# Token sum of pk summed ahead on VectorE, a Strassen product added in one place and taken away in another, the last tile in quarters, and new tables of order: a two-layer attention and FFN kernel on one core

## The chip, the cores and the metric

The kernel runs on one core of a Trainium2 chip. The metric is the device time of one execution in microseconds (us). Executions of one kernel differ by up to 1.7 us, so effects of a few tenths of a microsecond can't be read from times, only from traces.

Words used below: TensorE multiplies matrices, VectorE and ScalarE work on tiles elementwise, PSUM holds the matmul results in 8 banks. The **pitch** of a matmul is the distance from its start to the start of the next when nothing holds it up. A **matmul wait** is what a start-to-start distance has beyond the pitch. I summed such waits from the matmul starts of a trace, from 10 us on, with pitches of 216, 109, 56, 42 and 25 ns for 512, 256, 128, 96 and 1 columns. A **centring pass** subtracts a token's mean, a part of the layernorm.

## The reference

Twice the same block, on 2048 tokens of width 512, 32 heads of 16 features, an FFN of width 1376; all in bf16:

```python
def _A_ref(x, wqkv, wo):                       # linear attention
    q, k, v = split_heads(x @ wqkv)
    phi = lambda t: where(t > 0, t + 1, exp(t)) + 1e-6
    pq, pk = phi(q), phi(k)
    kv  = einsum("bhsd,bhse->bhde", pk, v)
    z   = einsum("bhsd->bhd", pk)              # the token sum
    num = einsum("bhqd,bhde->bhqe", pq, kv)
    den = einsum("bhqd,bhd->bhq", pq, z)[..., None] + 1e-6
    return merge_heads(num / den) @ wo
def _B_ref(x, w1, w2):                         # FFN
    return max(x @ w1, 0) @ w2
x = x + _A_ref(layernorm(x), wqkv, wo);  x = x + _B_ref(layernorm(x), w1, w2)     # twice
```

(Shortened: shapes, types and the setup of the inputs are left out.)

## The kernel before

All operations are listed once. A table then says in which order they are issued, which engine takes those that either may do (a ScalarE, d VectorE), and which PSUM bank each tile gets. The tables are the outcome of an earlier search, so a change of operations comes with new tables.

```python
ORDER = """
17 0 14 12 15 18 13 1 16 19 2 20 22 3 24 4 21 23 25 5 6 ... 32a ... 46d ...
"""                                     # cut: about 1580 entries
BANKS = ("01436013227545647545447755457477567567454276447564227521...")   # cut
```

All matmuls go through one helper, so in the profile they share a line (L540 before, L538 after) and are told apart by their tiles:

```python
def mm_group(mk, reads, writes, dur, name):
    def _emit(e, mk=mk):
        last = None
        for (o, l, r, st, sp, skip) in mk():
            last = e.matmul(o, l, r, start=st, stop=sp, skip_group_check=skip)
        return last
    return g.add(PE, _emit, reads, writes, dur, name=name)
```

The token sum multiplies each block of 128x128 of pk by a column of ones, for 16 tiles of 4 blocks; the result is masked into Zc, from which the denominators come:

```python
def a_z_acc(lo, hi, zb, first):
    ...                                 # cut: src(i, j), block j of tile i of pk
    def mk():
        return [(psv[:, zb, j:j + 1], src(i, j), ones[:, 0:1], first and i == lo and j == 0, i == NT - 1, True)
                for i in range(lo, hi) for j in range(4)]
```

Strassen's scheme replaces 8 block products by 7, with sums of blocks before and after. It is chosen per chunk of 512 tokens: `QSTR` for Q of the second layer, `HSTR` for the first FFN product of each layer:

```python
QSTR=(3,),  HSTR=[(1, 2, 3), (1, 2, 3)]        # cut from the parameters
hs = HSTR[layer // 2]
steps.append((t, None, lambda t=t: b_h_str(t, layer) if t in hs else b_h(t)))
```

The last FFN output tile is finished in two halves, each with its own store:

```python
prod("f4", summed(3), B21S, ("w2t", "b21-11"), c1, L, False)
if tail:
    rem(c1, l1, L, i1)
    out_half(i1, 0, c1)                 # DVE: residual; then the store, halves on SP and ACT
```

## Time and profile before

| what | before |
|---|---|
| time, median of 4 runs | 270.66 us |
| span of the profiled run | 268.3 us |
| TensorE, VectorE, ScalarE busy | 98%, 89%, 74% |
| TensorE's unbroken run of matmuls, start | 9.59 us |
| end of the last matmul's pitch | 265.27 us |
| matmul waits between these | about 2.1 us |

The last row needs a word. The distances give 6.67 us, but 21 matmuls have no record in this trace (1976 of TensorE against 1997 weight loads), and each, nearly all of 512 columns, leaves a false gap of 0.216 us; 6.67 - 21 x 0.216 = 2.1.

The main views of this profile stand in the prediction.

The end of the timeline:

```profile
265.16 0.27 PE L540 MATMUL ps<-w,big 96*128 96x256 bf16 x1
265.48 0.47 DVE L1138 SCALAR_TENSOR_TENSOR xn<-ps,rstdf,xres 128x256 bf16<-128x256 f32 x1
265.98 0.42 SPq L1141 DMA_DIRECT2D out_dram<-xn  x1
```

The last store is issued 0.71 us after the last matmul's pitch ended (265.16 + 0.11).

### The profile page before, as it was taken

To read this page: it belongs to the slowest core of one execution; us is meant where nothing else is said; L and a number is where in the kernel's file an instruction comes from. 1 tells how busy PE (TensorE), PEld (TensorE's weight loads), DVE (VectorE), ACT (ScalarE), POOL (GpSimd) and SP (SyncE) were. 2 spreads that over 40 slices of the span, in tenths; PEclk is the share of its full clock that TensorE was granted. 3 is DMA by queue.
4 is the path that set the end of the run, shared out by engine and by line. 5 is a ranking of instruction groups with operands and counts; after the bars stand their busy time and mean duration, and the time that the engine had idled before them with its cause. 6 is when DMAs were issued, how large, how long until landed. Compare 5 with 4: busy or idle time off the path is not lost.

```text
span 268.3 us, 5363 instructions
## 1 busy us (share of the span) xinstructions
PE 262.3 (98%) x1976; PEld 172.3 (64%) x1997; DVE 238.4 (89%) x650; ACT 199.2 (74%) x434; POOL 18.7 (7%) x30
## 2 busy tenths in 40 slices
PE   7999999999999999999999999999999999999995
PEld 2444454447556878778776664455457688888884
DVE  4999986999989999998999984799889989999884
ACT  3889955999978769688867987889996878725420
POOL 4021000000110002210011000000100100200000
PEclk9999999999999999999999999999999999999999
DMA  6955882245243024402204400224363232202004
GB/s 202 381 121 82 216 286 94 101 67 119 91 123 75 0 42 86 55 0 44 56 2 78 78 5 2 98 81 85 74 157 100 41 76 45 95 2 84 16 1 156
DMA packets 47482, 23.61 MB, mean 88 GB/s; under 512 B 36736, under 2 KB 46048, under 8 KB 47456
## 3 DMA queue, kind: packets, MB, share of 16 engines
q1 hardware_dynamic: 47312, 23.21, 34.1%
q8 instruction: 15, 0.25, 0.4%
q14 instruction: 11, 0.09, 0.1%
q10 hardware_dynamic: 144, 0.07, 0.1%
HBM read 11.21 MB, written 3.15 MB: 53 GB/s over the span
## 4 chain that ended last, share of the span: by engine, by line
PE 95%; DVE 2%; DMA 1%; issue 1%; ACT 0%
PE ps L540 95%; DMA xin<-in_A_x_dram 1%; DVE bst L447 1%; DVE xn L580 0%; DVE xn L1178 0%; PE ps L503 0%; DVE mv L448 0%; DVE Tb L511 0%; DVE xn L1138 0%; ACT lnv L1169 0%; ACT rstd L1171 0%
## 5 line engine op out<-in xcount | busy, mean ns | idle before, releaser
L547 ACT ACTIVATE sqscr<-xres 128x512 bf16<-128x512 f32 x48 | 30.4, 634 | 10.8 <-DVE xres L584 5.9
L522 ACT ACTIVATE escr<-ps 128x512 bf16<-128x512 f32 x52 | 30.7, 609 | 6.8 <-PE ps L540 6.4
L520 ACT ACTIVATE big<-ps 128x512 bf16<-128x512 f32 x52 | 30.9, 613 | 1.4 <-PE ps L540 1.3
L540 PE MATMUL ps<-big,xn 128*128 128x512 bf16 x121 | 29.4, 379 | 0.4
L540 PE MATMUL ps<-gw,big 128*128 128x512 bf16 x121 | 28.9, 379 | 0.4
L1027 ACT ACTIVATE big<-ps 128x512 bf16<-128x512 f32 (+1 forms) x44 | 22.9, 533 | 6.5 <-PE ps L540 5.7
L540 PE MATMUL ps<-Tb,wqkv 128*128 128x512 bf16 x112 | 27.0, 379 | 0.0
L540 PE MATMUL ps<-wqkv,Tb 128*128 128x512 bf16 x91 | 22.7, 379 | 0.7 <-ACT Tb L510 0.3
L526 DVE TENSOR_TENSOR big<-big,escr 128x512 bf16<-128x512 bf16 x52 | 21.2, 421 | 1.5 <-ACT big L520 0.8
L540 PE MATMUL ps<-w2s,big 128*128 128x256 f16 x160 | 22.1, 272 | 0.0
L540 PEld LDWEIGHTS ps<-big,xn 128*128 128x128 bf16 x128 | 12.1, 98 | 13.9 <-issue 0.7
L540 PE MATMUL ps<-w,big 128*128 128x256 f16 (+2 forms) x113 | 20.9, 302 | 0.0
L540 PEld LDWEIGHTS ps<-gw,big 128*128 128x128 bf16 x128 | 12.2, 98 | 13.4 <-issue 0.5
L1010 ACT ACTIVATE ps<-ps 128x512 f32<-128x512 f32 (+1 forms) x29 | 15.0, 518 | 6.5 <-DVE big L1048 2.6
L540 PE MATMUL ps<-w,xin 128*128 128x256 bf16 (+1 forms) x140 | 19.5, 273 | 0.0
L540 PE MATMUL ps<-xn,xin 128*128 128x256 f16 x128 | 19.4, 273 | 0.0
L540 PE MATMUL ps<-Tb,w 128*128 128x512 bf16 x80 | 18.8, 379 | 0.0
L540 PEld LDWEIGHTS ps<-Tb,wqkv 128*128 128x128 bf16 x112 | 10.6, 98 | 12.0 <-ACT escr L522 0.3
L524 DVE TENSOR_SCALAR escr<-escr 128x512 bf16<-128x512 bf16 x52 | 14.4, 286 | 4.3 <-ACT escr L522 4.2
L540 PE MATMUL ps<-xn,w 128*128 128x256 f16 x120 | 18.2, 273 | 0.0
L540 PE MATMUL ps<-Tb,wper 128*128 128x256 bf16 x120 | 18.2, 273 | 0.0
L540 PEld LDWEIGHTS ps<-w2s,big 128*128 128x128 bf16 x160 | 15.5, 98 | 4.0 <-DVE xres L1105 0.4
(166 smaller groups left out, 548.6 us busy)
## 6 DMA issues: line engine op xcount, KB each, us to landing
xn<-rdram SPq DMA_DIRECT2D x32, 128.0 KB
wqkv<-in_A_wqkv_dram SPq DMA_DIRECT2D x3, 512.0 KB, 7.3
xin<-in_A_x_dram SPq DMA_DIRECT2D x3, 512.0 KB, 8.1
out_dram<-xn SPq DMA_DIRECT2D x3, 512.0 KB, 2.8
w<-in_B_w_dram SPq DMA_DIRECT2D x1, 1376.0 KB, 6.6
w<-in_B_w_dram SPq DMA_DIRECT2D x1, 1280.0 KB, 9.8
rdram<-rsp SPq DMA_DIRECT2D x8, 128.0 KB, 1.7
wo<-in_A_wo_dram SPq DMA_DIRECT2D x1, 512.0 KB, 10.6
```

The source lines that it names most:

```text
L447: g.add(DVE, lambda e: e.bn_stats(bst[:, i, :], xin[:, i, :]), [("xin", i)] + list(behind), [("bst", i)], C_DVE_BNST, name="bnst%d" % i)
L520: g.add(ACT, lambda e: e.activation(dst_ap, psv[:, b, :], ACTF.Identity, bias=1.0 + 1e-6, scale=1.0), [("ps", b)], [dst_key], C_ACT_PSUM, ...
L522: g.add(ACT, lambda e: e.activation(escr[:, s, :], psv[:, b, :], ACTF.Exp), [("ps", b)], [("escr", s)], C_ACT_EXP, name=name + "_exp")
L524: g.add(DVE, lambda e: e.tensor_scalar(escr[:, s, :], escr[:, s, :], 1.0, 1e-6, ALU.min, ALU.add), [("escr", s)], [("escr", s)], C_DVE_BF4 ...
L526: g.add(DVE, lambda e: e.tensor_tensor(dst_ap, dst_ap, escr[:, s, :], ALU.max), [dst_key, ("escr", s)], [dst_key], 340.0, name=name + "_phi")
L540: last = e.matmul(o, l, r, start=st, stop=sp, skip_group_check=skip)
L547: g.add(ACT, lambda e: e.activation(sqscr[:, q, :], xres[:, i, :], ACTF.Square, accum_out=dst[:, i:i + 1]), [("xres", i)], [("sqscr", q), ...
L1010: g.add_flex([(ACT, lambda e: e.activation(dst(), psv[:, src, 0:W], ACTF.Identity), cost(C_ACT_PSUM)), (DVE, lambda e: e.tensor_copy(dst() ...
L1027: g.add_flex([(ACT, lambda e: e.activation(out_ap(r, m), pv(b), ACTF.Relu), cost(C_ACT_PSUM)), (DVE, lambda e: e.tensor_scalar(out_ap(r, m ...
```

## The change

The intent: give TensorE less to do where VectorE can take it. (1) In three chunks of the first layer and all four of the second, VectorE adds the four pk tiles of a chunk to one, in fp16, and only that one goes through the one-column matmuls. (2) The first FFN product of the last layer uses Strassen in chunk 0 as well. (3) Q of the second layer no longer does, which frees VectorE. (4) The last half of the last tile becomes two quarters. The tables of order and banks are new throughout.

```diff
-17 0 14 12 15 18 13 1 16 19 2 20 22 3 24 4 21 23 25 5 6 26 27 7 28 8 29 40 30 33 ...
+17 0 14 12 15 18 13 1 16 19 2 20 22 3 24 4 21 23 25 5 6 26 27 7 28 8 33 29 40 30 ...
 (cut: the rest of ORDER, and BANKS)
-QSTR=(3,), ..., ZP=(0, 0), ..., HSTR=[(1, 2, 3), (1, 2, 3)]
+QSTR=(),   ..., ZSUM=[(0, 1, 2), (0, 1, 2, 3)], ..., HSTR=[(1, 2, 3), (0, 1, 2, 3)]
-        def a_z_acc(lo, hi, zb, first):
+        def a_z_acc(t, zb):
+            ...                                     # cut: tiles, keys and src of the chunk
+            if t in ZSUM[cur_layer[0] // 2]:
+                zs = rhi[:].bitcast(F16)
+                hv = big[:].rearrange("p (c t k) -> p c t k", t=NCH, k=512)
+                ks = [("rhi", 0), ("rhi", 1)]
+                g.add(DVE, lambda e: e.tensor_tensor(zs, hv[:, 0:2, t, :], hv[:, 2:4, t, :], ALU.add), keys, ks, 608.0, name="zs%d" % t)
+                g.add(DVE, lambda e: e.tensor_tensor(zs[:, 0, :], zs[:, 0, :], zs[:, 1, :], ALU.add), ks, ks, 340.0, name="zt%d" % t)
+                src, keys = [zs[:, 0, :]], ks[0:1]
             def mk():
+                return [(psv[:, zb, j:j + 1], x[:, 128 * j:128 * j + 128], ones[:, 0:1], t == 0 and k == 0 and j == 0, t == NCH - 1, True)
+                        for k, x in enumerate(src) for j in range(4)]
-            prod("f4", summed(3), B21S, ("w2t", "b21-11"), c1, L, False)
             if tail:
-                rem(c1, l1, L, i1)
-                out_half(i1, 0, c1)
+                for q in range(2):
+                    cols = slice(128 * q, 128 * q + 128)
+                    prod("f4%d" % q, summed(3), B21S[:, :, cols], ("w2t", "b21-11"), c1, cols, False)
+                    rem(c1, l1, cols, i1)
+                    out_part(i1, cols, c1, q)
-                ... eng=(SP, ACT)[hf] ...            # queue of the store
+                ... eng=(SP, ACT, SP)[k] ...
 (cut: an unused path of the token sum on GpSimd, removed)
```

## The prediction

> **What bounds the kernel now.** I read the engine shares first, then the chain of waits, then TensorE's timeline for the pitch of each kind of matmul, and last VectorE and ScalarE by stage. The page's first two parts (busy microseconds, share of the span, instructions; then busy tenths in 40 slices) say that TensorE is never idle at full clock, and that VectorE is close behind:
>
> ```profile
> PE 262.3 (98%) x1976; PEld 172.3 (64%) x1997; DVE 238.4 (89%) x650; ACT 199.2 (74%) x434; POOL 18.7 (7%) x30
> ...
> PE   7999999999999999999999999999999999999995
> ...
> DVE  4999986999989999998999984799889989999884
> ACT  3889955999978769688867987889996878725420
> ...
> PEclk9999999999999999999999999999999999999999
> ```
>
> A busy TensorE is not yet a bound, because the profile models the ends of matmuls. The chain that ended last settles it: by line it is nearly all one matmul helper, and its pieces (start, length, what) run from 5 us to 265 us in blocks with gaps of about 0.05 us.
>
> ```profile
> by line: PE ps L540 94.9%; DMA xin<-in_A_x_dram 0.9%; DVE bst L447 0.9%; issue 0.6%; DVE xn L580 0.3%; DVE xn L1178 0.3%; PE ps L503 0.2%; DVE mv L448 0.2%; DVE Tb L511 0.2%; DVE xn L1138 0.1%; ACT lnv L1169 0.1%; ACT rstd L1171 0.1%
> ...
> 81.63 30.23 PE ps L540 x263
> ...
> 217.48 47.31 PE ps L540 x427
> 264.79 0.02 issue
> 264.81 0.75 DVE xn L580
> 265.56 0.39 DVE xn L1138
> ```
>
> So a matmul costs its pitch, the start of one block to the start of the next over the number of matmuls, not its listed duration. From TensorE's timeline:
>
> ```profile
> 39.80 5.35 PE L540 MATMUL ps<-big,xn 128*128 128x512 bf16 x24
> 44.99 0.38 PE L540 MATMUL ps<-Tb,wqkv 128*128 128x512 bf16 x1
> ...
> 46.72 1.06 PE L540 MATMUL ps<-gw,wqkv 128*128 128x128 bf16 x16
> 47.62 1.03 PE L540 MATMUL ps<-Tb,wqkv 128*128 128x512 bf16 x4
> ...
> 157.52 1.34 PE L540 MATMUL ps<-ones,big 128*128 128x1 bf16 x48
> 158.72 0.60 PE L540 MATMUL ps<-big,Tb 128*128 128x256 f16 x4
> 159.16 1.03 PE L540 MATMUL ps<-Tb,wqkv 128*128 128x512 bf16 x4
> ```
>
> 512 columns: (44.99-39.80)/24 = 216 ns. 256 columns: (159.16-158.72)/4 = 110 ns. 128 columns: (47.62-46.72)/16 = 56 ns. One column: (158.72-157.52)/48 = 25 ns. Counting all matmuls from 9.6 us to the last (575 of 512 columns, 1066 of 256, 36 of 128, 128 of 96 columns at 42 ns, 128 of one column, 8 denominator groups of 0.34 us) gives about 254 us against the 255.7 us that the trace shows. At most 2 us are stalls, and most of them are the small issue gaps. The kernel is a sum of matmul pitches plus a head of 9.6 us and a tail of 3 us.
>
> **What the Trainium skill says.** "TensorE: Matmul & The Clock Gate", section "Wait — 56ns, not 53.3ns?": a warm matmul takes N/2.4 GHz plus about 2.5 ns, and start to start never falls below about 25 ns. The trace agrees to the nanosecond: 216, 110, 56 and 25 ns. So a one-column matmul is nearly half as dear as one of 128 columns, and it is the number of them that counts. "VectorE: DVE Perf Modes", sections on the performance tiers and on the TRN2 errata: tensor_tensor on 16-bit data in SBUF handles two elements a cycle, and a SBUF operation costs 58 cycles and the elements over that rate at 0.96 GHz. That is 327 ns for 512 elements and 727 ns for 1280; in VectorE's timeline such sums start 0.335 and 0.73 us apart, so the trace agrees, and 1024 elements should take 0.60 us. "DMA: Bandwidth & Descriptors", section on the anatomy of one DMA: a fixed cost of about 2 us that doesn't shrink with the size. Here 128 KB landed 1.7 us after issue and 64 KB 1.6 us, so a smaller last store gains next to nothing. Its specification table adds that pieces under 512 B lose rate; quarter-width rows are 256 B. No store of that kind is in this trace.
>
> **The change part by part.**
>
> (1) Token sum of pk. Before, both attention layers sum 16 tiles with 4 one-column matmuls each: 128. After, chunks 0 to 2 of the first and all four of the second are first added on VectorE to one tile, so the matmuls are 3x4 + 16 = 28 and 4x4 = 16. TensorE loses 84 x 25 ns = 2.10 us. VectorE gains seven times one addition of 1024 elements (0.60, estimated above) and one of 512 (0.335): 6.6 us. In itself this lies beside the matmuls.
>
> (2) First FFN product of the last layer, chunk 0, by Strassen. Plain: 10 blocks x 4 = 40 matmuls of 512: 8.64 us. Strassen: 7 products x (4+4+2) = 70 of 256 at 109.4 ns: 7.66 us. TensorE loses 0.98 us. The weight sums exist already (made once in layer 1). Extra on VectorE: four sums of transposed tiles (1.34), three additions c21 and three hadd (0.61 full, 0.34 half size: 1.56 each), three small maxima (0.5): 5.0 us. On ScalarE or VectorE: 9 copies and 9 ReLU, each six full at 0.48 and three half at 0.28 (7.4 us together), in place of 10 ReLU (4.8): 2.6 us more.
>
> (3) Q of layer 2, chunk 3, without Strassen: from 28 x 109.4 ns = 3.06 us to 16 x 216 ns = 3.46: TensorE gains 0.40 us. VectorE is freed of five weight sums and four tile sums (9 x 0.335) and two additions on PSUM (0.6 each): 4.2 us. ScalarE is freed of three copies: 1.45 us.
>
> (4) Tail in quarters. The last half product of 5+1 matmuls of 256 (0.66 us) becomes two of 5+1 of 128 (0.67 us): nothing on TensorE. The end gets longer, as I read the new table of order. The last quarter's matmuls wait until VectorE has read the first quarter from the same bank; the product and remainder of tile 15 fill that wait. But tile 15's own output (0.67 us on VectorE) is placed just ahead of the last quarter's, and only 0.34 us of matmuls follow it. Before, the last store was issued at 265.98 us, 0.7 us after the last pitch ended (about 265.27). After, I get: last pitch T, tile 15's output from T-0.14 to T+0.53, quarter output (about 0.34) to T+0.87, then a store that queues behind that of tile 15 on the same issuer (about 0.4 us per issue in this trace): T+1.0. That is 0.3 us worse, an estimate.
>
> Sum on the path: -2.10 - 0.98 + 0.40 + 0.02 + 0.3 = -2.4 us, so 270.57 - 2.4 = 268.2 us. VectorE: +6.6 + 5.0 - 4.2 = +7.4 us, from 238 to about 246 in a span of 266 (92%). ScalarE: +1.2.
>
> **The rivals.**
>
> VectorE becomes the bound in a stage. Busy time by stretches of the kernel before:
>
> ```profile
> 145.00:165.00 20.00, 19.89 (x176) 12.46 (x177) 17.56 (x55) 17.90 (x36) 1.11 (x1) 1.00 0.14 28
> 165.00:190.00 25.00, 24.84 (x145) 12.40 (x147) 20.65 (x63) 21.39 (x44) 0.00 (x0) 1.00 0.27 75
> 190.00:215.00 25.00, 24.89 (x188) 16.11 (x189) 22.46 (x64) 21.32 (x51) 2.01 (x2) 1.00 0.42 99
> 215.00:240.00 25.00, 24.95 (x227) 21.03 (x226) 23.27 (x59) 16.29 (x38) 2.01 (x2) 1.00 0.23 56
> 240.00:265.00 25.00, 25.00 (x229) 20.84 (x227) 21.18 (x38) 8.36 (x20) 0.00 (x0) 1.00 0.15 53
> ```
>
> Columns after the length are TensorE, its weight load, VectorE, ScalarE, GpSimd. The sums of layer 2 (3.7 us) fall into 145 to 170 us, where 5 us are free and 1.7 us of Q's weight sums go away. The new Strassen chunk puts 5.0 us on VectorE and 2.6 on ScalarE in 190 to 215 us, where 2.5 and 3.7 are free: it doesn't fit there. It must draw on the 4 us free and the 2.5 us freed before, and move work that either engine may do to ScalarE, which has 8.7 us free in the next stretch. In sum it fits. If the order misses, TensorE waits for buffers: 1 to 2 us lost, 269 to 270. Against it: the kernel before runs VectorE above 9.5 of 10 for long stretches and shows hardly a matmul wait.
>
> The token sum sits on the path of its stage. The new order of work is then PSUM, exponential, maximum, two additions, matmul, mask, denominator; if the extra 1 us of latency delays the first denominator and nothing fills the gap, up to 1 us per attention layer comes back: 269 to 270. Against it: projections and accumulation matmuls are there to fill, and in the first layer the last chunk stays unsummed.
>
> The tail is better than I read it, or the whole order is a lucky one: 267.3 to 267.8.
>
> **Range and chances.** The matmul count is certain and its pitch measured, so -2.7 us before the tail is firm; nearly all doubt lies in new stalls, and they only add. Predicted 268.2 us, range 267.3 to 269.7. Faster by over 2% needs 265.2 or less, 3 us beyond what the matmuls can give: 0.02. Slower by over 2% needs over 7 us of new stalls: 0.01. Within 2%: 0.97.
>
> **What would show it.** Right: one-column matmuls 44 instead of 128 and still 25 ns apart; 70 more of 256 columns with FFN operands; VectorE's busy time near 246 us with TensorE's share unchanged; the fp16 additions starting 0.6 and 0.34 us apart; the last store issued about 1.0 us after the last matmul's pitch. Wrong: waits of matmuls for VectorE of over 0.3 us between 195 and 225 us or ahead of the first denominator groups; TensorE pieces in the chain interrupted by VectorE; a gain over 2.7 us, which would mean that the kernel before had hidden stalls that I took for pitch.

## More of the kernel before

The one-column matmuls of the token sum, from the view by tile of `ones` (count, then listed ns as minimum, median, maximum):

```profile
L540 PE MATMUL ps<-ones,big x128: 163/163/177, 18.4 to 163.9; 128*128 128x1 bf16 x128
```

The listed 163 ns is the way through the engine, not the cost: they follow each other at 25 ns. Next, from the timelines of the DMA queue and of TensorE, the transposes of the normalized tiles for the first FFN product, and the matmuls that read them first (start, length, what):

```profile
55.85 6.87 SPq L486 DMA_TRANSPOSE Tb<-xn  x4
...
65.27 2.85 PE L540 MATMUL ps<-Tb,w 128*128 128x512 bf16 x12
```

No idle time is noted in brackets behind the matmuls: the transposes, begun 9 us ahead, had landed.

## The result, and the profile after

| | before | after |
|---|---|---|
| time, median of 4 runs each | 270.66 us (270.08 to 270.93) | 268.37 us (268.26 to 269.12) |
| ratio | | 0.9924 (95%: 0.9899 to 0.9948) |
| the same again, 11 and 6 runs | 270.40 us | 268.80 us, ratio 0.9932 (0.9911 to 0.9954) |
| span of a profiled run | 268.3 us | 267.4, again 266.7 us |

A ratio is the mean time of the one kernel's runs over the mean of the other's runs of the same rounds, so it is not quite the ratio of the medians beside it. The gain is 0.7 to 0.8%, some 2 us, which counts as the same within 2%. The profile of the first line's runs fell on their slowest one (269.12 us), so I read the second profile of the same kernel (run of 268.47 us, all 1937 matmuls recorded). First the page's engine line:

```profile
PE 261.4 (98%) x1937; PEld 171.7 (64%) x1937; DVE 240.5 (90%) x660; ACT 202.3 (76%) x446; POOL 19.6 (7%) x30
```

TensorE is as full as before, with 60 instructions fewer (1997 - 84 + 70 - 40 - 28 + 16 + 6 = 1937: the one-column matmuls, the FFN product, Q, the quarters). VectorE rose by 2 us only. The token sum in the first profile of the changed kernel, by the tiles `ones` and `rhi` (the sums lie in `rhi`):

```profile
L538 PE MATMUL ps<-ones,rhi x28: 163/163/167, 34.2 to 165.0; 128*128 128x1 bf16 x28
L538 PE MATMUL ps<-ones,big x16: 163/163/163, 38.8 to 39.2; 128*128 128x1 bf16 x16
L616 DVE TENSOR_TENSOR rhi<-big x7: 680/686/693, 29.1 to 162.5; 128x1024 f16<-128x1024 bf16 x7
L617 DVE TENSOR_TENSOR rhi<-rhi x7: 417/420/426, 31.4 to 163.3; 128x512 f16<-128x512 f16 x7
```

128 one-column matmuls became 44, and seven pairs of additions came. The same rule of reading holds for VectorE: 686 ns is listed, but the next operation starts 0.60 to 0.61 us later. Two rows of busy time by stretch answer to the prediction's (TensorE, weight load, VectorE, ScalarE, GpSimd after the length):

```profile
145.00:165.00 20.00, 20.00 (x133) 11.27 (x132) 19.24 (x54) 17.89 (x36) 0.00 (x0) 1.00 0.14 28
...
190.00:215.00 25.00, 25.00 (x226) 19.77 (x224) 23.78 (x65) 23.13 (x57) 1.01 (x1) 1.00 0.52 96
```

In the stage of the second token sum VectorE went from 17.56 to 19.24 us of 20, and in the stage of the new Strassen chunk from 22.46 to 23.78 of 25. There is little left of either, and TensorE's column shows no hole. The hole is elsewhere. Pieces of the chain that ended last (start, length, what):

```profile
10.01 49.41 PE ps L538 x272
...
60.53 0.61 ACT xn L556
...
61.47 4.75 DMA Tb<-xn
66.22 0.05 issue
66.27 27.54 PE ps L538 x189
...
93.83 0.76 DVE xres L582 x2
...
102.17 0.38 ACT ps L1104
...
102.59 160.74 PE ps L538 x1288
```

Before, the chain ran through these times in one piece after another of TensorE:

```profile
48.79 10.31 PE ps L540 x49
59.10 0.05 issue
59.16 15.46 PE ps L540 x109
```

Now it leaves TensorE at 59.4 us, goes through a centring pass on ScalarE and the transpose of that tile by DMA, and returns at 66.27. The timelines of the queue and of TensorE show the same:

```profile
55.21 2.87 SPq L484 DMA_TRANSPOSE Tb<-xn  x2
...
60.11 2.62 SPq L484 DMA_TRANSPOSE Tb<-xn  x2
...
66.27 1.90 PE L538 MATMUL ps<-Tb,w 128*128 128x512 bf16 x8 [0.82 <-DMA Tb<-xn]
```

Before, four transposes were issued in one go from 55.85 us. In the new order two of them come at 60.11 us, after a late centring pass, and the matmuls that read them wait (0.82 us idle by the profile, 0.99 us against the pitch). A smaller wait of 0.31 us stands at 102.2 us, at the entry to the first FFN's second product, where the kernel before had 0.09 us; there the chain runs for 8.8 us, from 93.8 to 102.6 us, mostly through VectorE.

**The sum.** From the start of TensorE's unbroken run to the end of the last pitch the kernel before took 265.27 - 9.59 = 255.7 us and the changed one 263.64 - 9.62 = 254.0 us: 1.7 us less. The matmuls removed are worth 2.10 + 0.98 - 0.40 - 0.02 = 2.66 us. So 1.0 us of new waits came, which is what the waits themselves say: 3.2 us against 2.1. Last, the end of the timeline after:

```profile
263.31 0.45 PE L538 MATMUL ps<-w,xin 128*128 128x128 f16 x5
...
263.60 0.22 PE L538 MATMUL ps<-w,big 96*128 96x128 bf16 x1
264.02 0.34 DVE L1134 SCALAR_TENSOR_TENSOR xn<-ps,rstdf,xres 128x128 bf16<-128x128 f32 x1
...
264.40 0.37 ACTq L1138 DMA_DIRECT2D out_dram<-xn  x1
```

The last pitch ends at 263.60 + 0.04; the store follows 0.76 us later, on ScalarE's queue.

### The profile page after: what moved, and what is told of

Read it like the earlier page. It is cut to its first block, busy times and chain, and to the rows that moved or that the text cites. A ratio compares the mean times of both kernels' runs of the same rounds, so it can differ in the third digit from the quotient of the medians.

```text
span 267.4 us, 5269 instructions
## 1 busy us (share of the span) xinstructions
PE 260.0 (97%) x1919; PEld 171.5 (64%) x1937; DVE 240.7 (90%) x660; ACT 202.4 (76%) x446; POOL 19.6 (7%) x30
## 4 chain that ended last, share of the span: by engine, by line
PE 85%; DVE 7%; DMA 5%; issue 1%; ACT 1%; SPq 0%; DVEq 0%
PE ps L538 84%; DMA Tb<-xn 3%; DMA xin<-in_A_x_dram 1%; DVE xres L551 1%; DVE xres L582 1%; DVE ps L1035 1%; DVE xn L970 1%; DVE xin L1061 1%; DVE xn L558 0%; ACT big L518 0%; PE ps L501 0%; DVE xn L578 0%; DVE bst L445 0%; DVE KVT L649 0%; ACT xn L556 0%
## 5 line engine op out<-in xcount | busy, mean ns | idle before, releaser
L520 ACT ACTIVATE escr<-ps 128x512 bf16<-128x512 f32 x56 | 33.3, 614 | 7.1 <-PE ps L538 7.0
L1021 ACT ACTIVATE big<-ps 128x512 bf16<-128x512 f32 (+1 forms) x57 | 29.2, 530 | 8.0 <-PE ps L538 7.7
L518 ACT ACTIVATE big<-ps 128x512 bf16<-128x512 f32 x56 | 33.3, 611 | 1.4 <-PE ps L538 1.3
L538 PE MATMUL ps<-Tb,wqkv 128*128 128x512 bf16 x128 | 30.5, 379 | 0.0
L538 PE MATMUL ps<-xn,w 128*128 128x256 f16 x140 | 21.8, 273 | 0.0
L538 PE MATMUL ps<-w,big 128*128 128x256 f16 (+3 forms) x114 | 21.6, 301 | 0.0
L538 PE MATMUL ps<-Tb,wper 128*128 128x256 bf16 x140 | 21.3, 272 | 0.0
L538 PEld LDWEIGHTS ps<-big,xn 128*128 128x128 bf16 x128 | 12.0, 97 | 13.1 <-issue 0.7
L571 POOL TENSOR_TENSOR rstdf<-varf,nhalf 128x4 f32<-128x4 f32 x8 | 9.6, 1201 | 145.1 <-DVE varf L569 145.1
L538 PE MATMUL ps<-w,xin 128*128 128x256 bf16 (+2 forms) x145 | 19.7, 269 | 0.1
L1104 ACT ACTIVATE ps<-ps 128x256 f32<-128x256 f32 x27 | 10.0, 371 | 11.8 <-PE ps L538 10.3
```

Source lines behind the costliest of these rows:

```text
L518: g.add(ACT, lambda e: e.activation(dst_ap, psv[:, b, :], ACTF.Identity, bias=1.0 + 1e-6, scale=1.0), [("ps", b)], [dst_key], C_ACT_PSUM, ...
L520: g.add(ACT, lambda e: e.activation(escr[:, s, :], psv[:, b, :], ACTF.Exp), [("ps", b)], [("escr", s)], C_ACT_EXP, name=name + "_exp")
L571: g.add(POOL, lambda e: e.tensor_tensor(rstdf[:, sl], varf[:, sl], nhalf[:, 0:4], ALU.pow), [("varf", t), ("nhalf",)], [("rstdf", t)], C_P ...
L1021: g.add_flex([(ACT, lambda e: e.activation(out_ap(r, m), pv(b), ACTF.Relu), cost(C_ACT_PSUM)), (DVE, lambda e: e.tensor_scalar(out_ap(r, m ...
L1104: g.add_flex([(ACT, lambda e: e.activation(psv[:, c1, cols], psv[:, c2, L], ACTF.Identity), 290.0), (DVE, lambda e: e.tensor_copy(psv[:, c ...
```

## The experiments

**Theory.** The time is the sum of the matmul pitches; the change takes 2.66 us of them away, and its new order has about 1.0 us more waits. **Rivals:** VectorE at its limit (the additions cost TensorE time, so their saving is partly given back); the tail in quarters costs or gains; the gain comes from the new order alone and not from the operations. Three calls were made, each with eleven runs of the kernel before beside it (medians 270.40, 270.38 and 270.35 us); ratios are against these.

### The changed kernel again

No edit. It is the baseline of the other runs.

> The changed kernel unaltered, timed again in five rounds as the yardstick for the parts. If the matmul count sets the time and the first profile's 1 us wait for a transposed tile was chance, the ratio to the kernel before is about 0.9915 (2.3 us less) and that wait is absent or shorter. If the wait belongs to the schedule, it shows again near 62 us with about 1 us.

Measured: 268.80 us, ratio 0.9932, as in the table above. The gain is repeatable, and so is the wait for the transpose near 65 us (0.82 us idle by the profile, 1.0 us in the first one): by the expectation's own test it belongs to the order.

### The token sum without the additions

The new order, but every tile goes through the one-column matmuls again:

```diff
-ZSUM=[(0, 1, 2), (0, 1, 2, 3)]
+ZSUM=[(), ()]                       # and the 14 entries of the additions taken out of ORDER
```

> The changed kernel with the pk tiles summed by TensorE again in both layers: 84 one-column matmuls more, seven pairs of VectorE additions (6.6 us) fewer, everything else in its place. Theory (TensorE's count is the bound): 84 x 25 ns = 2.1 us slower than the changed kernel. Rival (VectorE is the bound in the stages of the sums): the freed 6.6 us of VectorE pay part of it back, under 1.2 us slower.

Measured: 271.15 us, ratio 1.0015 (0.9991 to 1.0039), 2.35 us above the changed kernel by the medians; 84 x 25 ns are 2.10 us. All of the token sum's saving arrives, and without it the rest of the change is level with the kernel before. Page line and TensorE's timeline of this run:

```profile
PE 263.7 (98%) x2021; PEld 174.1 (65%) x2021; DVE 234.9 (87%) x646; ACT 202.6 (75%) x446; POOL 19.7 (7%) x30
...
66.62 2.75 PE L537 MATMUL ps<-Tb,w 128*128 128x512 bf16 x12
```

Two things are to be seen. VectorE is 5.6 us less busy, so the seven pairs cost 5.6 us of busy time. And the matmuls that read the transposes start at 66.62 us with no wait for them. Yet its matmul waits sum to 3.1 us, as in the changed kernel: they lie elsewhere (0.8 us at 60 to 70 us, 0.6 us at 190 to 210 us). So the extra microsecond of waits belongs to the new order; the additions didn't bring it.

### The additions kept, the matmuls put back as idle ones

This separates the two halves of that trade. Behind each summed chunk 12 one-column matmuls are added whose results nobody reads, 84 in all:

```diff
+                if len(src) == 1:
+                    mms += [(psv[:, zb, 8 + j:9 + j], src[0][:, 128 * j:128 * j + 128], ones[:, 0:1], False, t == NCH - 1, True)
+                            for r in range(3) for j in range(4)]
```

> The changed kernel with 84 idle one-column matmuls added behind the sums, into columns that nobody reads; VectorE's work is unchanged. Theory: 84 x 25 ns = 2.1 us slower. Rival (the matmuls hide in waits for VectorE or the denominator): under 1 us slower. The difference from the run with direct sums is what the VectorE additions cost by themselves: 0 by the theory.

Measured: 271.19 us, ratio 1.0024 (0.9998 to 1.0050): 2.39 us for 84 matmuls, 28 ns each by the medians, with an uncertainty of about half a microsecond in all. A one-column matmul costs its pitch, end to end. The run differs from the one above only in having the additions and in the operand of the matmuls, and the two medians are 0.04 us apart: 5.6 us of VectorE's busy time cost nothing measurable.

### The larger addition twice

The rival in its own coin: each of the seven sums does its addition of 1024 elements once more.

```diff
+g.add(DVE, lambda e: e.tensor_tensor(zs, hv[:, 0:2, t, :], hv[:, 2:4, t, :], ALU.add), keys, ks, 608.0, name="zr%d" % t)
```

> The changed kernel with the 1024-element addition done twice in each of the seven sums: 4.2 us more VectorE work, TensorE unchanged. Theory (VectorE has room in these stages): within 0.3 us. Rival (VectorE is at its limit there, and the change's own additions already cost time): 1 to 4 us slower, with matmuls waiting for VectorE between 25 and 40 us or 150 and 165 us.

Measured: 272.17 us, ratio 1.0053 (1.0031 to 1.0075), 3.37 us above the changed kernel for 7 x 0.60 = 4.2 us more of VectorE. The waits of matmuls (total us, times, longest):

```profile
PE ps L538 <- DVE rhi L618: 1.0, 2, 0.5
PE ps L538 <- DVE xn L971: 1.0, 1, 1.0
PE ps L538 <- DMA Tb<-xn: 1.0, 1, 1.0
PE ps L538 <- DVE big L524: 0.8, 1, 0.8
```

TensorE now waits for the sums themselves (`rhi`), at 167 us, ahead of the second layer's first denominators, for a phi product on VectorE (`big`) and at 201 us for a sum of transposed tiles (`xn`); the wait for the DMA is the old one. Waits sum to 7.2 us against 3.2. The theory's "within 0.3 us" missed. So the rival is false for the change as it stands and true for 4 us more: the additions just fit.

### The tail in halves

The new order with the last half product in one piece:

```diff
-                for q in range(2):
-                    cols = slice(128 * q, 128 * q + 128)
-                    ...                                   # cut: the quarter's product, remainder, output
+                prod("f4", summed(3), B21S, ("w2t", "b21-11"), c1, L, False)
+                rem(c1, l1, L, i1)
+                out_part(i1, L, c1, 1)
```

> The changed kernel with its last product in one half of 256 columns instead of two quarters, everything else in its place. My prediction took the quarters for 0.3 us of loss, since it had the last store queue behind another on one issuer; the first trace shows it on an issuer of its own, 0.7 us after the last matmul, as before. Theory now: within 0.2 us of the changed kernel, and the 0.16 us wait ahead of the last quarter's matmuls gone. If the first reading was right after all: 0.3 us faster. If the quarters help: 0.2 us or more slower.

Measured: 268.87 us, ratio 0.9935 (0.9909 to 0.9962), against 268.80 and 0.9932. Its end:

```profile
264.05 0.27 PE L538 MATMUL ps<-w,big 96*128 96x256 bf16 x1
...
264.88 0.38 ACTq L1136 DMA_DIRECT2D out_dram<-xn  x1
```

The store follows the last pitch (264.05 + 0.11) by 0.72 us; with quarters it was 0.76. With quarters there is also a wait of 0.17 us ahead of the last product, for VectorE's read of the first quarter from the same bank, which is absent here. So by the traces quarters cost some 0.2 us; in the times no difference shows.

### The token sum alone, in the old order

The kernel before with the seven pairs of additions, each put right behind the last tile it needs; Q, FFN product, tail and the rest of the order as before.

```diff
-a_z_acc over all 16 tiles
+ZSUM=[(0, 1, 2), (0, 1, 2, 3)]      # additions inserted into the old ORDER
```

> The kernel before with the summed pk tiles as the only part of the change, its order otherwise kept. By the matmul count alone: 2.1 us faster than the kernel before. Since doubled additions cost 3.4 us, I now expect VectorE to take most of it back where the order was not made for it: 0 to 1.5 us faster, with matmul waits for VectorE near the sums, and the waits are to show that the new order is a part of the gain.

Measured: 277.51 us, ratio 1.0245 (1.0217 to 1.0273): slower by 7 us, with 2.1 us less work for TensorE. One such place in TensorE's timeline:

```profile
39.43 0.25 PE L537 MATMUL ps<-ones,rhi 128*128 128x1 bf16 x4 [1.57 <-DVE rhi L616]
```

The additions for this chunk ran at 38.15 and 38.95 us, just ahead of the matmuls, which stood in front of all later matmuls in TensorE's queue. Matmul waits sum to 13.1 us. That is 10.9 us more than before; less the 2.1 us of work it makes 8.8 us, as the spans have it (277.1 against 268.3 us).

Not all of that is waiting. TensorE's granted clock, in 40 slices of this run:

```profile
PEclk9999998999999999999999997999999999999999
```

It was half from 40.4 to 43.9 us and from 166.7 to 170.2 us, so about 3 of the 13.1 us are slower matmuls. In the 3.4 us just before each of the two stretches TensorE had been busy for only 1.75 and 1.05 us, held up by the waits. The one run of six with a mean clock of 1.0 took 276.15 us, 5.8 us above the kernel before; the others had 0.988 to 0.994.

So the operations without the order lose, and the order without the additions gains nothing (1.0015, above): the rival "the order alone" falls, and put into the old order this plainly the operations gain nothing.

### The FFN product without Strassen in chunk 0

```diff
-HSTR=[(1, 2, 3), (0, 1, 2, 3)]
+HSTR=[(1, 2, 3), (1, 2, 3)]         # order and banks redone around it by plain list placement
```

> The changed kernel with chunk 0 of the last layer's first FFN product computed plainly again (40 matmuls of 512 columns instead of 70 of 256), banks and order redone only there. Theory (count of matmuls): 1.0 us slower than the changed kernel, about 269.8. Rival (the 5 us on VectorE and 2.6 on ScalarE that Strassen adds cost time in 190 to 215 us): less than 0.5 us slower, or even faster.

Measured: 285.37 us, ratio 1.0542 (1.0516 to 1.0567). Waits rose to 19.5 us (about 3 of them slower matmuls, in two stretches at half clock), nearly all between 180 and 240 us, where I had redone the order. The test is spoiled by my order and tells nothing of the 0.98 us end to end. That figure rests on the count (40 matmuls of 512 columns against 70 of 256) and on the pitches, which are the same in both traces.

### The centring pass and the transposes earlier

The wait at 65 us attacked directly: ten entries of the order moved, so that the late centring pass and its transposes come earlier; all operations unaltered.

```diff
 ORDER: entries of nmf1, cen1, tr0, nmf2, nmf3, cen3, cen2, tr2 and one sum of tiles moved ahead;
        one product (wa1_2) moved behind wa1_1
```

> The changed kernel with ten entries of its order moved: the weight sum wa1_2 behind wa1_1, and the centring of tiles 1 to 3 with their transposing stores ahead of it, so that the second transpose of chunk 0 is issued about 0.8 to 1.2 us earlier. If the 1.0 us wait near 65 us is set by that issue, it shrinks below 0.3 us and the kernel gains 0.7 to 1.0 us: about 267.8. If the wait is set by something else (traffic of other transfers, the producing matmuls), the gain is under 0.3 us.

Measured: 268.58 us, ratio 0.9922 (0.9901 to 0.9944), 0.2 us below the changed kernel's median and within its interval. The wait for the transposes is gone, but see the product ahead of it in TensorE's timeline:

```profile
65.38 0.61 PE L538 MATMUL ps<-xn,xin 128*128 128x256 f16 x4 [0.37 <-DVE nm2f L565]
...
66.26 2.10 PE L538 MATMUL ps<-Tb,w 128*128 128x512 bf16 x9
```

The matmuls that read the transposes start at the same 66.26 us. TensorE now waits elsewhere instead, mostly for VectorE, 1.1 us in this stretch against 1.3. That moving one pass up moved others down, with VectorE busy for 9.6 us of the 10 from 60 to 70 us (in the changed kernel), is argued, not shown: the kernel before has 9.7 us there and no such wait.

### Other orders for the same operations

Could an order searched anew separate the parts? I searched one for the kernel before, for the changed one, for the token sum alone and for the changed one without Strassen in chunk 0, with the kernel's own replay of durations and somewhat slower hand-overs between engines.

> The kernel before, its operations unaltered and only the order of issue searched anew (by the kernel's own replay of its order with slower hand-overs between engines). The kernel before has hardly any matmul waits left, so an order cannot give much: within 0.4 us of it. If it is over 1 us faster, the gain of the change was mostly its new order and not its smaller matmul count.

> The kernel before plus the summed pk tiles alone, order searched as in the run before this one. By the matmul count: 2.1 us faster than the kernel before. If the 6.6 us of additions don't fit VectorE as long as Q of layer 2 is still by Strassen (4.2 us of VectorE work), part is lost again: 0.5 to 1.5 us faster, with matmul waits for VectorE near 160 us.

> The changed kernel with chunk 0 of the last layer's first FFN product plain, order searched in the same way; it takes the place of the earlier attempt, whose order was bad. By the count of matmuls: 1.0 us slower than the next run. If Strassen's extra work on VectorE and ScalarE costs time there: 0.5 us slower or less.

> The changed kernel, its operations unaltered, order searched in the same way. Its matmul waits in the trace come to 1.0 us near 65 us, 0.3 near 102 us and 0.2 us at the end. If the order can hide them: 0.7 to 1.3 us faster than the changed kernel, about 267.7, and the fastest of all. If they only move: within 0.3 us.

| operations | tuned order | order searched anew | ratio of that to before |
|---|---|---|---|
| before | 270.35 us | 281.74 us | 1.0413 (1.0395 to 1.0430) |
| token sum alone | none | 282.32 us | 1.0413 (1.0380 to 1.0447) |
| changed, plain FFN chunk 0 | none | 278.37 us | 1.0304 (1.0262 to 1.0346) |
| changed | 268.80 us | 276.37 us | 1.0215 (1.0195 to 1.0235) |

(The 268.80 us are from the first call.) Where there is a tuned order, mine is slower by 11.4 and 7.6 us. Waits of matmuls in the last run:

```profile
PE ps L538 <- DVE big L524: 3.0, 4, 1.2
```

TensorE waits at 11 to 65 us for the phi products on VectorE (`big`), which my replay had thought ready. By the medians the token sum alone shows no gain over its partner (waits of 14.4 us against 11.9), and the plain FFN chunk is 2 us slower than its partner. But these medians mix clocks. The profiled run of the token sum alone has two stretches of 3.4 us at half clock (8.7 to 12.1 and 25.7 to 29.1 us), and four of its six runs (282.07 to 282.72 us) have a mean clock of 0.988. Its two runs at 0.998 and 1.0 took 279.95 and 280.33 us, the three of its partner at 0.999 or more 281.37 to 281.94 us: about 1.6 us faster, of the 2.1 us of the count. Likewise the plain FFN chunk at 0.999 or more (277.46 to 277.70 us) against its partner at 0.998 or more (275.75 and 276.16 us): 1.6 us slower, where the count says 0.98. So few runs, of orders that differ, agree with the counts in sign but don't prove their sizes; as a clean separation the runs miss. What they do show is the size of the order's part: four to six times that of the whole change.

No run beats the changed kernel clear of noise.

## Why the prediction was right or wrong

Predicted were 268.2 us; 268.37 and 268.80 us came. The total lies within the range in both, and the verdict of the same within 2% held. By its steps:

- **The bound.** Right. TensorE is full in both kernels, and 84 idle matmuls of one column cost about what the pitch says (28 ns each for 25). By the traces the gain was 1.7 us, not 2.4; that the first median lies only 0.2 us from the prediction is in part the luck of the runs, since the second lies 0.6 us off.
- **Token sum, -2.10 us.** Right, shown by two runs (2.35 and 2.39 us). Its cost on VectorE was given as 6.6 us from the start-to-start distances; the busy time rose by 5.6 us.
- **FFN product, -0.98 us, and Q, +0.40 us.** Right as counts at unchanged pitches. No run isolates either end to end: the one for the FFN product was spoiled by its order, and Q was not tried. Nor do the times show them: without the additions the changed kernel is level with the one before, so what these parts save is no more than the new order's waits take back.
- **Tail, +0.3 us.** Mis-sized, and for another reason than given. I wrote that the last store "queues behind that of tile 15 on the same issuer". It is on ScalarE's queue, and tile 15's output starts 0.29 us ahead of the last pitch's end instead of 0.14, so the store comes 0.76 us after it, not 1.0. But I also had the last quarter's wait for its bank filled by tile 15's product and remainder, and 0.17 us of it stays. Together about 0.2 us, and not visible in the times.
- **The failed step: "nearly all doubt lies in new stalls, and they only add", with no term for them in the sum.** About 1.0 us came, 0.17 of it that of the tail. I had looked for them between 195 and 225 us and ahead of the denominators. The largest is at 65 us, in a stage whose operations the change doesn't touch: a late centring pass, a late transpose. I read the order table for the tail only. One of the prediction's own signs of being wrong, the chain leaving TensorE for VectorE, did appear from 93.8 to 102.6 us, but only 0.31 us of waiting came of it. A term of 1 us in place of the tail's 0.3 would have given 270.57 - 2.66 + 1.0 = 268.9 us.
- **Rival "VectorE becomes the bound".** Not at the change's size, but 4.2 us more of it cost 3.4 us. Near, as the figures given there had it: if all of the second layer's additions fall into 145 to 165 us, 17.56 + 3.7 - 1.7 = 19.6 us of 20, and 19.24 was measured. (Free between 145 and 170 us were 6.1 us, not the 5 that the prediction states: 2.44 before 165 us and 3.64 after.)
- **VectorE's busy time, 246 us.** 240.5 us were measured. In part the additions added less than priced (5.6 for 6.6). In part work that either engine may do went to ScalarE: its operations that take a Strassen result from PSUM with ReLU rose from 44 to 57, where the change has only 9 more, and its busy time rose by 3.1 us instead of 1.2.
- **Rival "the token sum sits on the path of its stage".** In the changed order not: between 30 and 50 us, the waits are about what they were. In the old order with the additions put in plainly it happened, with single waits of up to 1.9 us.

What stays open: why just this order has the late centring pass. It came out of a search, and a search that minimizes a modelled time can place a wait where the model sees none; that is argued, not shown.

## What to carry to other kernels

Where TensorE is full, price a change by counting matmuls times pitch, and test that price by adding idle ones: 84 of one column cost 2.4 us. Then read the new order at every place where data comes from another engine or by DMA, in untouched stages too, because a stall costs as much as forty small matmuls and no count shows it. And when a part is undone for an experiment, the order must be remade as well as it was made, or the experiment measures the order: here orders were worth 8 to 11 us and the change 2. And compare runs at the same granted clock: with the token sum alone in the searched order, the runs at a mean clock of 0.988 took 1.7 to 2.8 us longer than those at 0.998 or more, as much as the whole change gains.

## What the Trainium skill lacked or had wrong

- "TensorE: Matmul & The Clock Gate", section "Wait — 56ns, not 53.3ns?": N/2.4 GHz and 2.5 ns with a floor near 25 ns hold here where the granted clock was full, but for the denominators: the four matmuls of such a group, of 512 columns and on 32 columns of the array each, start 3 ns apart. It doesn't say that the floor counts end to end: 84 idle one-column matmuls cost 2.39 us, 28 ns each, in a full TensorE.
- "VectorE: DVE Perf Modes", section on the TRN2 errata: it gives a fixed cost of 58 cycles and, as measured for a single operation, about 150, and this section doesn't say which to use for back-to-back work (another page of the skill does). Both show here: a sum of 1024 elements is listed with 686 ns (659 cycles, 147 above 512) and the next starts after 0.60 to 0.61 us (64 to 74 above).
- "DMA: Bandwidth & Descriptors": beside figures of rate it has no time from issue to landing for an on-chip transpose of a tile of 128x512 (elsewhere the skill has one duration, for 128x128). Here the median is 3.2 us for 30 transposes, and the one that TensorE waited for took 4.75 us in the chain. For its warning on pieces under 512 B: the last stores of 32 KB in rows of 256 B landed 1.6 to 1.7 us after issue, like those of 128 KB, so at this size no loss shows.
- On no page that I read: how much a tuned order of issue is worth when all operations stay the same. Here 281.74 against 270.35 us, and 276.37 against 268.80 us.
- On no page that I read: how much TensorE may wait within a stretch before its clock is halved for the next. In the traces here seven stretches of 3.4 us at half clock each follow 3.4 us in which TensorE was busy for 1.05 to 1.80 us; one with 1.71 us, in the order searched anew for the kernel before, was followed by full clock, so this share alone doesn't decide it.
